# A gated linear attention with a ReLU feed-forward on one core: new issue orders, with one unit's y and two transposes ahead of the first gates

## The chip, the cores and the metric

The kernel runs on one core of a Trainium2 chip. The metric is the device time of one execution in microseconds (us); the time of a kernel is the median of its runs. The core's engines run side by side: TensorE (PE, with its weight loads as PEld), VectorE (DVE), ScalarE (ACT), GpSimd (POOL) and SyncE (SP), each with its own in-order queue of instructions, and transfers (DMA) that SP, ACT and POOL issue.

## What is computed

Four batches, eight heads, 768 positions, head size 48. The first half is a recurrence with a decay for each row of the state, the second a feed-forward with a ReLU gate over 3072 tokens of width 384 and a hidden width of 1536:

```python
def _attn_ref(q, k, v, f_logit):
    f = 1.0 / (1.0 + np.exp(-f_logit))
    state = zeros((B, H, D, D)); y = zeros_like(q)
    for t in range(S):
        state = f[:, :, t, :, None] * state + einsum('bhd,bhe->bhde', k[:, :, t], v[:, :, t])
        y[:, :, t] = einsum('bhd,bhde->bhe', q[:, :, t], state)
    return y

x = attn_out.transpose(0, 2, 1, 3).reshape(B * S, H * D)
gate = np.maximum(x @ w_gate, 0.0)
out = (gate * (x @ w_val)) @ w_out
```

## The kernel before

The recurrence is done in chunks of 128 positions. A step is one (chunk, batch) pair; 24 steps stand in six groups of four, written as group c = 0 to 5 and place b = 0 to 3. The first eight steps are paired into four units, which work on two neighbouring chunks of one batch at once, so places 0 and 1 of group 0 are one unit ("unit 0" by its number, with its two halves b = 0, 1; the steps b = 2, 3 of group 0 belong to the second unit; the change's own words call these steps unit 0's second half, and so does this text). For a step, in this order:

- the logits are loaded (L...f), ScalarE makes log(1 + exp(-f)) (`ef`, `ln`), TensorE sums it over positions with a triangular matrix (`cum`), ScalarE takes the exponentials (`ek`, `eq`) and the decay over the chunk (`dc`);
- GpSimd or VectorE multiply k and q with them, which gives the tensors `hats` (`hk`, `hq`). The first eight steps turn them on TensorE (`tk`, `tq`) and copy them from PSUM to SBUF (`ck`, `cq`); the others by transposing DMAs (`xh`);
- TensorE makes the scores (`s`), VectorE masks them (`m`), TensorE makes y within the chunk (`y`) and from the state (`yi` in a unit), and the chunk's share of the state (`kv`), which VectorE and GpSimd add and scale (`st`, `ss`, `sd`);
- y is copied into xT (`x`), or copied (`n`) and turned by DMA (`xx`), and is then the feed-forward's input.

The feed-forward works on a group of 512 tokens, the first one's first four hidden blocks on 256 tokens at a time. For hidden block j of 12, TensorE makes the gate (`g`) and the value (`u`) from slices of w_gate and w_val, ScalarE or VectorE the ReLU (`r`), VectorE the product (`p`); `o` are the output steps (four matmuls each), `d` their copies and `S` the stores. A name such as g02.1 is the gate of group 0 from place 2 on, block 1; u00.3 a value, o02.4 the output of place 2 over blocks 4 to 7. Weights are fetched in slices by DMAs that GpSimd issues: wg0+2 is w_gate's blocks 0 and 1, wv4+4 w_val's 4 to 7, wo4+8 w_out's 4 to 11. Loads of f, k, q and v are issued by SyncE, later ones also by ScalarE.

All of this is added to a plan as numbered operations, in one order; what runs when is set by tables. `ORDER` lists for each engine the numbers in the order of its queue (a negative entry ~12512 stands for 12 dummy matmuls of 512 columns that keep TensorE busy), `BANKS` gives the PSUM bank of each accumulation in TensorE's order, and `HELD` adds three waits by hand (69: 185 makes wv8+4 wait for relu r00.6). An operation's engine follows from the list it stands in. The waits are worked out from these lists: an engine waits for another only where data or a buffer asks for it, and everything behind a waiting instruction on its queue waits too.

```python
tenant, at = {}, 0
for op in self.order["PE"]:
    for t in op.opens:
        place = places[at]
        at += 1
        for o in tenant.get(place, ()):
            if op.deps.get(o, "order") == "order":
                op.deps[o] = "war"
        tenant[place], t.ap = t.ops, banks[place]
```

So a step that opens a bank waits for the last reader of that bank's tenant before it.

Of the kernel before, what the change touches and what calls it, by code (L numbers as in the profile page):

```python
# [25 lines left out]

ORDER = {
    "PE": [
        45, ~12512, 85, 74, ~2512, 90, ~2512, 121, 110, 80, ~2512, 82, 92, 95, 128, 101, ~9512, 116, 118, 266, 126,
# [14 lines left out]
    ],  # L44
    "ACT": [
# [9 lines left out]
    ],  # L55
    "DVE": [
# [11 lines left out]
    ],  # L68
    "POOL": [
# [4 lines left out]
    ],  # L74
# [5 lines left out]
    ],  # L80
}

# [2 lines left out]
}  # L85

BANKS = [
# [9 lines left out]
]  # L97


# [895 lines left out]
```

## Time and profile before

| | us |
|---|---|
| median of 3 runs | 191.91 (190.73 to 192.16) |
| the profiled execution | 190.59 |
| its span, first to last instruction | 188.9 |
| TensorE busy | 182.4 (97%) |
| VectorE busy | 133.9 (71%) |
| ScalarE busy | 91.9 (49%) |
| GpSimd busy | 60.7 (32%) |
| granted TensorE clock | 1.000 |

The profile is of one execution. The busy time of an engine leaves out its register, branch and DMA-issuing instructions; the end of a matmul is modelled, so that neighbouring matmuls overlap. DMA shares and landing times are of the core's 16 DMA engines. In the profile's rows, L842 is the gate and value matmul, L721 and L757 y of a unit, L699 its scores, L744 its state share, L601 the transposes, L589 and L590 the hats on GpSimd and VectorE, L443 the weight DMAs, L411 the loads of the units, L646 the copy to xT.

### The profile page before, as it was taken

What the parts mean: (1) busy time and instruction counts of PE and PEld (TensorE: products, weight loads), DVE (VectorE), ACT (ScalarE), POOL (GpSimd) and SP (SyncE); (2) the same over time, 40 slices, a digit from 0 to 9 for tenths busy, and PEclk for the clock granted to TensorE, in tenths of its full rate; (3) what the DMA queues carried; (4) which work ended last, traced back from release to release, by engine and by line L of the source; (5) the groups of instructions that cost most, each with busy time, mean ns of one, the idle gap of its engine ahead of it and who ended that gap; (6) DMA issues with size and microseconds to landing.
All of it is one profiled execution on the core that took longest, in us unless ns stands there. A gap on an engine that the chain in (4) does not pass through costs nothing.

```text
span 188.9 us, 4607 instructions
## 1 busy us (share of the span) xinstructions
PE 182.4 (97%) x1902; PEld 104.9 (56%) x1902; DVE 133.9 (71%) x246; ACT 91.9 (49%) x179; POOL 60.7 (32%) x88
## 2 busy tenths in 40 slices
PE   7989699999999999999999999999999999999994
PEld 3446486555545556555566555665555665555562
DVE  4476977988268879669776977997689954447802
ACT  3998746266882764866821648361425201240211
POOL 7099892600368210690018750126020000000000
PEclk9999999999999999999999999999999999999999
DMA  5999999997999999979899799795991120020223
GB/s 155 325 304 274 267 273 200 218 211 156 234 184 257 207 183 237 224 146 164 194 232 177 185 191 191 142 186 117 257 271 41 23 63 3 0 83 0 82 89 125
DMA packets 111045, 32.44 MB, mean 172 GB/s; under 512 B 104240, under 2 KB 110768, under 8 KB 111024
## 3 DMA queue, kind: packets, MB, share of 16 engines
q1 hardware_dynamic: 82128, 23.87, 58.2%
q10 hardware_dynamic: 25152, 4.73, 13.4%
q0 software_dynamic: 3744, 3.54, 11.3%
q8 instruction: 15, 0.25, 0.6%
q14 instruction: 6, 0.05, 0.1%
HBM read 25.95 MB, written 4.72 MB: 162 GB/s over the span
## 4 chain that ended last, share of the span: by engine, by line
PE 86%; DMA 6%; SPq 3%; POOL 2%; ACT 1%; issue 0%
PE ps L842 49%; PE ps L863 25%; DMA wg<-in_moe_w_gate_dram 3%; SPq L411 3%; DMA f_in<-in_f_logit_dram 3%; PE ps L633 2%; PE ps L795 2%; POOL hats L589 2%; PE ps L524 1%; PE ps L822 1%; PE ps L721 1%; PE ps L601 1%; PE ps L806 1%; PE ps L802 1%; PE ps L699 1%; PE ps L757 0%
## 5 line engine op out<-in xcount | busy, mean ns | idle before, releaser
L850 DVE TENSOR_TENSOR gT<-relu,ps 128x512 bf16<-128x512 bf16 (+1 forms) x76 | 48.0, 655 | 18.8 <-ACT relu L847 9.3
L842 PE MATMUL ps<-xT,wv 128*128 128x512 bf16 (+1 forms) x228 | 56.1, 368 | 0.0
L842 PE MATMUL ps<-xT,wg 128*128 128x512 bf16 (+1 forms) x228 | 54.7, 368 | 1.2 <-DMA wg<-in_moe_w_gate_dram 1.1
L863 PE MATMUL ps<-wo,gT 128*128 128x384 bf16 (+2 forms) x300 | 53.9, 320 | 0.0
L847 ACT ACTIVATE relu<-ps 128x512 bf16<-128x512 f32 (+1 forms) x47 | 26.7, 577 | 49.0 <-PE ps L842 46.7
L863 PEld LDWEIGHTS ps<-wo,gT 128*128 128x128 bf16 x300 | 28.1, 98 | 20.0
L842 PEld LDWEIGHTS ps<-xT,wg 128*128 128x128 bf16 x228 | 23.7, 108 | 21.3 <-DMA wg<-in_moe_w_gate_dram 1.5
L842 PEld LDWEIGHTS ps<-xT,wv 128*128 128x128 bf16 x228 | 23.5, 108 | 18.9
L848 DVE TENSOR_SCALAR relu<-ps 128x512 bf16<-128x512 f32 (+1 forms) x29 | 18.9, 658 | 9.7 <-PE ps L842 9.6
L589 POOL TENSOR_TENSOR hats<-k_in,expk 128x384 bf16<-128x384 f32 x17 | 16.9, 999 | 26.2 <-ACT expk L546 26.1
L589 POOL TENSOR_TENSOR hats<-q_in,expq 128x384 bf16<-128x384 f32 x15 | 17.8, 1190 | 19.0 <-ACT expq L548 12.5
L641 DVE TENSOR_TENSOR ptm<-ps,tri 128x512 bf16<-128x512 f32 x32 | 20.3, 683 | 2.3 <-PE ps L633 2.1
L869 ACT ACTIVATE osb<-ps 128x384 f32<-128x384 f32 (+2 forms) x18 | 8.6, 480 | 22.1 <-PE ps L863 20.7
L548 ACT ACTIVATE expq<-ps 128x384 f32<-128x384 f32 x24 | 15.5, 669 | 0.0
L468 POOL TENSOR_TENSOR st<-ssum,dec 128x384 bf16<-128x384 f32 x9 | 8.5, 945 | 19.5 <-DVE ssum L466 19.5
L546 ACT ACTIVATE expk<-ps 128x384 f32<-128x384 f32 x24 | 11.8, 498 | 2.0 <-PE ps L524 1.3
L493 ACT ACTIVATE f_in<-f_in 128x768 f32<-128x768 f32 x12 | 10.1, 840 | 2.7 <-DMA f_in<-in_f_logit_dram 2.6
L706 DVE TENSOR_TENSOR ptm<-ps,tmask 128x512 bf16<-128x512 f32 x16 | 10.3, 683 | 1.1 <-PE ps L699 1.1
L496 ACT ACTIVATE bneg<-f_in 128x768 bf16<-128x768 f32 x12 | 10.0, 840 | 0.9 <-ACT relu L847 0.7
L646 ACT ACTIVATE xT<-ps 128x384 bf16<-128x384 f32 x10 | 5.1, 535 | 9.6 <-PE ps L795 5.9
L619 POOL CAST vpad<-v_in 128x384 bf16<-128x384 f32 x12 | 6.9, 588 | 8.9 <-DMA v_in<-in_v_dram 8.9
L466 DVE TENSOR_TENSOR ssum<-ps,st 128x384 f32<-128x384 f32 x16 | 8.8, 551 | 0.7 <-PE ps L822 0.6
(76 smaller groups left out, 150.1 us busy)
## 6 DMA issues: line engine op xcount, KB each, us to landing
out_dram<-osb SPq DMA_DIRECT2D x23, 192.0 KB, 2.2
q_in<-in_q_dram SPq DMA_DIRECT2D x10, 384.0 KB, 5.4
f_in<-in_f_logit_dram SPq DMA_DIRECT2D x9, 384.0 KB, 5.3
v_in<-in_v_dram SPq DMA_DIRECT2D x9, 384.0 KB, 5.9
k_in<-in_k_dram SPq DMA_DIRECT2D x8, 384.0 KB, 5.9
k_in<-in_k_dram ACTq DMA_DIRECT2D x4, 384.0 KB, 6.0
f_in<-in_f_logit_dram ACTq DMA_DIRECT2D x3, 384.0 KB, 5.5
v_in<-in_v_dram ACTq DMA_DIRECT2D x3, 384.0 KB, 3.8
```

The source lines that it names most:

```text
L493: add(f"ef{c}{b0}", by("ACT", lambda: sc.activation(raw, raw, AF.Exp, scale=-1.0), act_(n)), keys, keys, key=P)
L496: add(f"ln{c}{b0}", by("ACT", lambda: sc.activation(bo, fl, AF.Ln, bias=1.0), act_(n)), keys + [f"bneg{bi}"], [f"bn{bi}_{x % 2}" for x in ...
L546: add(f"ek{c}{b}", by("ACT", lambda: sc.activation(ex[1], parts(bc.ap[:, 0:HD]), AF.Exp, scale=1.0), act_(HD)), [bc], [f"expk{ei}"], key=P ...
L548: add(f"eq{c}{b}", by("ACT", lambda: sc.activation(ex[0], parts(bc.ap[:, 0:HD]), AF.Exp, scale=-1.0), act_(HD)), [bc], [f"expq{eqi}_{b % 2 ...
L589: return {**by("POOL", lambda: gp.tensor_tensor(o, i_, e_, ALU.mult), pool_(HD)), **by("DVE", lambda: ve.tensor_tensor(o, i_, e_, ALU.mult ...
L641: add(f"m{c}{b}{j}", by("DVE", lambda b=b, j=j, mi=mi: ve.tensor_tensor(ptm[mi][:, j, :, :], s[b, j].ap[:, :].rearrange("p (n t) -> p n t" ...
L706: add(f"m{c}{b2[i]}{j}", by("DVE", lambda i=i, j=j, mask=mask: ve.tensor_tensor(ptm[mi[i]][:, j, :, :], s[j, i].ap[:, :].rearrange("p (n t ...
L842: z = te.matmul(bank.ap[:, 0:n], wt[:, kt, w_cols(j)], xT[xi][:, kt, n0:n1], start=(kt == 0), stop=(kt == NK - 1))
L847: add(f"r{c}{b0}.{j}", {**by("ACT", lambda: sc.activation(rdst, gate.ap[:, 0:n], AF.Relu), act_(n)), **by("DVE", lambda: ve.tensor_scalar_ ...
L848: **by("DVE", lambda: ve.tensor_scalar_max(rdst, gate.ap[:, 0:n], 0.0), dve_(n))}, [gate], [f"relu{ri}"], key=P)
L850: add(f"p{c}{b0}.{j}", by("DVE", lambda: ve.tensor_tensor(gT[gi][:, j, n0:n1], rdst, val.ap[:, 0:n], ALU.mult), dve_(n)), [val, f"relu{ri} ...
L863: z = te.matmul(o.ap[:, 0:e1 - e0], gT[gi][:, j, b * C:(b + 1) * C], wo[:, j, e0:e1], start=(j == 0), stop=(j == NJ - 1))
```

## The change

Only the tables change: the lists of all five engines in `ORDER` and the places in `BANKS`; `HELD`, the operations and their instructions stay, and so does the number of dummy matmuls (27). By the lists, 19 operations go from GpSimd to VectorE and 15 back, 5 from GpSimd to ScalarE and 4 back, 35 from VectorE to ScalarE and 35 back (copies and relus in the main), 5 DMA issues from SyncE to ScalarE and 6 back. The first rows of the table for TensorE show its kind:

```diff
     "PE": [
-        45, ~12512, 85, 74, ~2512, 90, ~2512, 121, 110, 80, ~2512, 82, 92, 95, 128, 101, ~9512, 116, 118, 266, 126,
...
+        45, ~12512, 85, 74, ~2512, 90, ~2512, 121, ~2512, 82, 92, 80, 110, 101, 95, 128, ~9512, 116, 230, 118, 266,
```

TensorE, where group 0's first gates start. Names in the rows are the tiles written and read: ps<-ptm,vpad is y within the chunk, ps<-qkT,st_0 its part from the state, ps<-ident,hats a transpose step, ps<-xT,wg a gate, ps<-xT,wv a value, ps<-bneg,ident a cum, ps<-vpad,hats the state share kv02. Before, from cum11 on:

```order
L513 MATMUL ps<-bneg,ident 128x384
L744 MATMUL ps<-vpad,hats 128x96 x16
L842 MATMUL ps<-xT,wg 128x256 x6
L601 MATMUL ps<-ident,hats 128x128 x4
L842 MATMUL ps<-xT,wv 128x256 x6
L513 MATMUL ps<-bneg,ident 128x384
L842 MATMUL ps<-xT,wg 128x256 x6
L721 MATMUL ps<-ptm,vpad 32x128 x64
L757 MATMUL ps<-qkT,st_0 32x128 x12
L601 MATMUL ps<-ident,hats 128x128 x8
```

and in the change (its lines are numbered one higher), from cum11 on, behind g00.2:

```order
L514 MATMUL ps<-bneg,ident 128x384
L843 MATMUL ps<-xT,wg 128x256 x3
L745 MATMUL ps<-vpad,hats 128x96 x16
L843 MATMUL ps<-xT,wv 128x256 x3
L602 MATMUL ps<-ident,hats 128x128 x4
L843 MATMUL ps<-xT,wv 128x256 x3
L514 MATMUL ps<-bneg,ident 128x384
L602 MATMUL ps<-ident,hats 128x128 x4
L722 MATMUL ps<-ptm,vpad 32x128 x64
L758 MATMUL ps<-qkT,st_0 32x128 x12
L602 MATMUL ps<-ident,hats 128x128 x4
L843 MATMUL ps<-xT,wg 128x256 x12
```

The first six gate matmuls before are g00.3 and g00.2 (slice wg2+2), the next six g00.0 and g00.1 (slice wg0+2). In the change y02, yi03 and the transposes tk11 and tk12 stand ahead of g00.1 and g00.0, which are followed by g02.2 and g02.1; kv02 stands behind the gates of slice wg2+2 and no longer ahead of them.

GpSimd, where the weights of blocks 4 to 11 are issued; the bracket is what the instruction waits for (d_q2_0 is the landing of Lq1.0, d_q3_0 of Lq1.2, e_ACT a step of ScalarE). Before:

```order
L443 DMA wv<-in_moe_w_val_dram 128x3x512
L589 TENSOR_TENSOR hats<-q_in,expq 128x8x48
L443 DMA wg<-in_moe_w_gate_dram 128x3x512
L332 MEMSET vpad 128x4x16
L443 DMA wo<-in_moe_w_out_dram 128x2x768
L589 TENSOR_TENSOR hats<-q_in,expq 128x8x48 [waits d_q2_0]
L443 DMA wv<-in_moe_w_val_dram 128x3x512 [waits e_ACT]
L443 DMA wo<-in_moe_w_out_dram 128x2x1536
```

and in the change:

```order
L444 DMA wv<-in_moe_w_val_dram 128x3x512
L590 TENSOR_TENSOR hats<-k_in,expk 128x8x48 [waits d_k3_0,e_ACT]
L590 TENSOR_TENSOR hats<-q_in,expq 128x8x48 [waits d_q3_0]
L590 TENSOR_TENSOR hats<-q_in,expq 128x8x48 [waits e_ACT]
L333 MEMSET tri 128x128
L590 TENSOR_TENSOR hats<-q_in,expq 128x8x48 [waits d_q2_0]
L444 DMA wg<-in_moe_w_gate_dram 128x3x512
L590 TENSOR_TENSOR hats<-q_in,expq 128x8x48
L444 DMA wo<-in_moe_w_out_dram 128x2x768
L444 DMA wv<-in_moe_w_val_dram 128x3x512 [waits e_ACT]
L444 DMA wo<-in_moe_w_out_dram 128x2x1536
```

wv4+4 is now issued ahead of the hats of unit 3, and the hats that wait for Lq1.0 (hq10) stand ahead of wg8+4, the next (hq11) ahead of wo0+4.

SyncE's loads of the units, before:

```order
L411 DMA k_in<-in_k_dram 128x8x96 x2
L411 DMA q_in<-in_q_dram 128x8x96
L411 DMA v_in<-in_v_dram 128x8x96
L411 DMA q_in<-in_q_dram 128x8x96
L411 DMA v_in<-in_v_dram 128x8x96
```

and in the change:

```order
L412 DMA k_in<-in_k_dram 128x8x96 x2
L412 DMA q_in<-in_q_dram 128x8x96 x2
L412 DMA v_in<-in_v_dram 128x8x96 x2
```

Lq1.0 is issued one place earlier, ahead of Lv1.2.

103 rows, old and new, of tables (BANKS, ORDER) are left out of this document.

## The prediction

> **What bounds the kernel now.** I first cut the span into stretches and read the table of busy time by stage, then the order of time on TensorE in the one stretch that shows idle time, then the chain that ended last, then the transfers.
>
> By stage (columns: start and end, length, then busy us and instruction count of PE, PEld, DVE, ACT, POOL, then the granted clock, DMA share and GB/s):
>
> ```profile
> 6.20:18.20 12.00, 11.02 (x220) 6.82 (x220) 7.63 (x18) 10.91 (x25) 8.78 (x11) 1.00 1.22 297
> 18.20:23.30 5.10, 3.43 (x69) 2.25 (x67) 4.75 (x9) 4.27 (x12) 4.60 (x8) 1.00 1.29 271
> 23.30:46.00 22.70, 22.64 (x374) 14.53 (x375) 19.01 (x37) 11.18 (x22) 9.14 (x13) 1.00 1.14 217
> 46.00:186.20 140.20, 140.17 (x1236) 79.55 (x1234) 100.13 (x162) 62.07 (x118) 34.78 (x37) 1.00 0.75 149
> ```
>
> From 46.00 to 186.20 TensorE is busy 140.17 of 140.20 us at a granted clock of 1.00: it is the bound, and an order that issues the same matmuls can gain nothing there, only lose. What is left behind 186.20 is the last copy and store. Idle time is left in two rows: 0.98 us in 6.20:18.20 and 1.67 us in 18.20:23.30. Before 18.20 TensorE fills its waits with dummy matmuls, whose number the change keeps (27), so the second row is the one to read closely. TensorE there:
>
> ```profile
> 19.48 0.52 PE L744 MATMUL ps<-vpad,hats 64*128 64x96 bf16 x16 [0.29 <-POOL vpad L619]
> 19.93 0.83 PE L842 MATMUL ps<-xT,wg 128*128 128x256 bf16 x6
> 20.97 0.38 PE L601 MATMUL ps<-ident,hats 128*128 128x128 bf16 x4 [0.21 <-POOL hats L589]
> 21.19 0.82 PE L842 MATMUL ps<-xT,wv 128*128 128x256 bf16 x6
> 21.85 0.33 PE L513 MATMUL ps<-bneg,ident 128*128 128x384 bf16 x1
> 23.30 0.83 PE L842 MATMUL ps<-xT,wg 128*128 128x256 bf16 x6 [1.13 <-DMA wg<-in_moe_w_gate_dram]
> ```
>
> The row at 23.30 is gates g00.0 and g00.1, the first users of weight slice wg0+2, which lands there: TensorE stood 1.13 us for it. The chain that ended last says the same, and gives lengths of single steps (start, us, what):
>
> ```profile
> 16.77 6.49 DMA wg<-in_moe_w_gate_dram
> ...
> 24.13 0.66 PE ps L721 x62
> 24.80 0.28 PE ps L757 x12
> ...
> 27.68 0.22 PE ps L601 x4
> 27.90 0.98 PE ps L842 x9
> ...
> 29.39 2.43 PE ps L842 x12
> 31.82 0.57 PE ps L699 x32
> 32.39 0.33 PE ps L601 x4
> 32.72 0.65 PE ps L842 x3
> ```
>
> So an intra-chunk y of a unit is 0.66 us, its state part 0.28, one transpose step 0.22 (the 0.33 row carries a change of mode besides), a 256-wide gate or value step 0.33 (0.98 for three), a score step of a unit 0.57, a 512-wide step 0.65.
>
> **Part 1: four steps in front of the first gates.** Behind cum13 (the row at 21.85) the change puts tk11, y02, yi03 and tk12 ahead of g00.1 and g00.0. They are 0.22 + 0.66 + 0.28 + 0.22 = 1.38 us of work that used to stand behind the wait. Whether they can run before wg0+2 lands at 23.25 is a question of their inputs. What feeds the steps before them, y00 and yi01, changes in one point: of the two k hats of unit 0's second half the first stays on GpSimd behind the same k load, the second goes to VectorE. Its cost is in the bound of part 3. GpSimd there:
>
> ```profile
> 15.98 0.84 POOL L468 TENSOR_TENSOR st<-ssum,dec 128x384 bf16<-128x384 f32 x1
> ...
> 20.83 0.99 POOL L589 TENSOR_TENSOR hats<-k_in,expk 128x384 bf16<-128x384 f32 x1
> 21.77 0.81 POOL L443 DMA_DIRECT2D wg<-in_moe_w_gate_dram  x1
> ```
>
> xT of unit 0 leaves ScalarE in two copies instead of one each on ScalarE and VectorE, whose rows are
>
> ```profile
> 17.86 0.60 ACT L646 ACTIVATE xT<-ps 128x384 bf16<-128x384 f32 x1
> 18.30 0.49 ACT L548 ACTIVATE expq<-ps 128x384 f32<-128x384 f32 x1
> ```
>
> with 0.44 us from start to start, so the second ends near 18.9 to 19.0. The first gate g00.2 can start at 19.0; before, gates started at 19.93 behind a state step that waited. From there: g00.2, cum11, g00.3, kv02 to about 20.4, u00.3 held for a bank until ScalarE has read cum11's sums, behind the two copies and four more steps of 0.4 (near 20.7), tk10 21.0, u00.2 21.2, cum13 21.5. tk11 needs the hats that end at 20.83 + 0.99 = 21.8 in both orders; y02 needs a bank that VectorE frees near 22.0; then 22.05 + 0.66 + 0.28 + 0.22 = 23.2. All four fit. Term: minus 1.38 at that point, with a small wait left.
>
> The next weight stops part of it. wg0+2 may be issued up to 0.45 us later, because the state product of the row at 15.98 now reads beside VectorE's hats; that shift is not priced, since the following slice, wg4+4, decides: the row at 21.77 (issue) and the landing times by transfer (line, queue, count, KB, us to landing) say 21.77 + 7.5 = 29.27.
>
> ```profile
> v_in<-in_v_dram SPq DMA_DIRECT2D x1, 384.0 KB, 8.5
> ...
> wg<-in_moe_w_gate_dram POOLq DMA_DIRECT2D x1, 384.0 KB, 7.5
> ...
> wg<-in_moe_w_gate_dram POOLq DMA_DIRECT2D x1, 384.0 KB, 8.2
> wo<-in_moe_w_out_dram POOLq DMA_DIRECT2D x1, 384.0 KB, 10.1
> ```
>
> Before, its first user g00.5 starts at 29.39 (the row of the chain). In the change g00.4 starts at 29.3, and s12 (0.57), tq10 (0.22) and u02.1 (0.33) have been done by then that were not: 1.12, and 0.1 for the start, so **minus 1.2 us** stands at 29.3.
>
> **Part 2: GpSimd's weight issues.** GpSimd before:
>
> ```profile
> 26.76 0.80 POOL L443 DMA_DIRECT2D wg<-in_moe_w_gate_dram  x1
> 27.56 0.17 POOL L332 MEMSET vpad<- 128x64 bf16 x1
> 27.65 0.74 POOL L443 DMA_DIRECT2D wo<-in_moe_w_out_dram  x1
> 28.93 0.99 POOL L589 TENSOR_TENSOR hats<-q_in,expq 128x384 bf16<-128x384 f32 x1 [0.54 <-DMA q_in<-in_q_dram]
> ```
>
> The change puts hq10, which waits for the q load of unit 2 (Lq1.0), ahead of wg8+4, and hq11 ahead of wo0+4; queued behind that wait are also wv8+4 and wo4+8, and who waits for them are gates 8 to 11 and the first output steps. SyncE issues that load one place earlier, in the place of a v load:
>
> ```profile
> 17.25 2.41 SPq L411 DMA_DIRECT2D v_in<-in_v_dram  x1
> 19.70 1.15 SPq L411 DMA_DIRECT2D q_in<-in_q_dram  x1
> ```
>
> The v load landed at 17.25 + 8.5 = 25.8; the q load before landed at 28.9, where the hats started. So hq10 finds its data when GpSimd comes to it, near 26.4 (hats of 1.0 each from 23.3 on), wg8+4 is issued near 27.4 (0.65 later than before) and wo0+4 near 29.2 (1.5 later). Need: g00.10 comes eight 512-wide steps, one transpose and one score step after 29.3: 29.3 + 5.2 + 0.22 + 0.67 = 35.4; o02.0 four steps later, 38.0. Upper end, if a landing follows its issue by the same time as before: wg8+4 at 27.4 + 8.2 = 35.6 (0.2 late), wo0+4 at 29.2 + 10.1 = 39.3 (1.1 later than 38.2): 1.3 us. Lower end: nothing, if the slices stand in line: before, these two were issued 0.9 us apart and landed at 35.0 and 37.7, 2.7 apart, so the second was waiting for the first and not for its issue. I take **plus 0.2**, near the lower end, since the gap of 2.7 against 0.9 is the nearest row.
>
> The Trainium skill, "DMA: Bandwidth & Descriptors", section "Queues, rings and completion order", says that on each DMA engine the descriptors of one ring are consumed in ring order while the engine takes turns between rings. By that rule a slice in a backlogged ring loses nothing by a later issue, and the sum would be 0.2 lower; the landings 2.7 us apart agree. That the weights' larger backlog (wv4+4 is issued right behind wg4+4) then takes turns from the q load is the same rule against this change; no run so far shows its size.
>
> wv8+4 and wo4+8 wait for r00.6 by a written hold; that relu moves forward with TensorE, so they are issued no later: nothing.
>
> **Part 3: the rest.** Exchanges of copies, relus and hats between VectorE, ScalarE and GpSimd (35 pieces each way between VectorE and ScalarE) lie beside a full TensorE. What hides them is the 140.17 us row; VectorE has 100.13 of 140.20 there, so 40 us of slack in the mean. Taken at nothing; if one arrives late, its lateness is added one to one. Upper bound by the nearest row: 1 us, the wait that one missing transfer caused at 23.30. The first stretch is also taken at nothing, between minus 0.5 (half of its 0.98) and plus 0.5 (one more hats on VectorE).
>
> **Sum.** The profiled execution took 190.59 (span 188.9 and 1.7 around it). 190.59 - 1.2 + 0.2 = 189.6. The runs shown have a median 1.3 above the profiled one, so I forecast **190.9** for a median. One per cent is 1.9 us, about what a measurement of this kernel can tell from no change; the whole idle time of 18.20:23.30 is less than that.
>
> **Rivals.** *A, slower: GpSimd stands at the q load in front of the weights.* If Lq1.0 lands when it did before (28.8), hq10 ends at 29.9, wg8+4 lands at 29.9 + 8.2 = 38.1, 2.7 late; hq11 and wo0+4 follow, issued at 31.7, landing at 41.8 against a need of 38.1 + 2.6 = 40.7, 1.1 more. 190.59 - 1.2 + 3.8 = 193.2, median 194.5. It outweighs the gain once hq10 starts after about 26.4, if landings follow issues. For it: the 0.54 us wait in the row at 28.93. Against it: the earlier place on SyncE. *B, the transfers hide the gain:* issue to landing stays 8.2 and 10.1, 1.3 us come back as waits for wg8+4 and wo0+4, 190.7, median 192.0. For it: wg0+2, which set the chain. Against it: 2.7 against 0.9. *C, faster:* all 1.67 us of the second row and half of the first's 0.98 go: 188.4, median 189.7. For it: all waits there lie on transfers or banks that the new order uses later. Against it: g00.2 still waits for xT, and wg4+4 for its landing.
>
> **How the numbers follow.** Forecast 0.52, B 0.20, A 0.15, C 0.13. C, which ends beyond the bound of 190.0, and the lower edge of the forecast give faster by over 1%: 0.16. Most of A, and a little for a stall that I have not seen, give slower by over 1%: 0.15. Within 1%: 0.69. The range runs from 189.2, below C, to 193.8, one per cent above the runs of before: it leaves out the far part of A and a little below C. The forecast's own range is 190.0 to 191.8.
>
> **What would show it.** Right: the 1.13 us wait in front of the first wg gate is under 0.5, with y and two transposes ahead of it; TensorE's idle time between 18.2 and 30 us falls by about 1; wg8+4's user starts by 35.6; 46 us to the end is as full as before, and ends 1 us earlier. Wrong: a wait of TensorE on DMA wg or wo between 35 and 42 us (B; A, with GpSimd idle on q_in ahead of it), or idle time of more than 0.5 us in any stretch behind 46 us, where I saw none.

## The result

The change has a median of 189.63 us (6 runs), against 191.38 for the kernel before in the 6 runs beside it; the ratio is 0.990, 95% interval 0.986 to 0.994. In a second set it was 189.62, ratio 0.990 (0.984 to 0.996). Ratios leave out executions more than 1.5% above the fastest of the same kernel, while medians hold them all.

The profiled execution took 189.74 (span 188.0), 0.85 less than the profiled 190.59 of before. The medians differ by 1.8. So there are two questions: whether the 0.85 is where the prediction put it, and where the other microsecond comes from.

The table of the change by stage (start and end, length, then busy us and count of PE, PEld, DVE, ACT, POOL, the clock, DMA share, GB/s):

```profile
6.20:18.20 12.00, 10.96 (x220) 6.89 (x222) 9.31 (x20) 11.21 (x26) 6.65 (x9) 1.00 1.22 302
18.20:23.30 5.10, 4.15 (x138) 3.04 (x134) 4.30 (x8) 4.39 (x13) 3.93 (x6) 1.00 1.27 267
23.30:46.00 22.70, 22.03 (x324) 14.49 (x320) 17.49 (x34) 12.42 (x25) 10.24 (x15) 1.00 1.08 207
```

TensorE's idle time in 18.20:23.30 fell from 1.67 to 0.95 us. From 18.2 to 30 us it fell from 1.73 to 1.09, less than the 1 us that the prediction named as its sign. The 0.67 of the third row must be read with care: this trace holds 1882 of the 1902 matmuls, and a missing first matmul of a step looks like 0.2 us of idle time. A profile with all 1902, shown further down, has none there. Behind 46 us TensorE shows no wait for another engine or a transfer in this trace, only three gaps of up to 0.2 us put down to "issue". TensorE itself:

```profile
19.32 0.50 PE L843 MATMUL ps<-xT,wg 128*128 128x256 bf16 x3 [0.53 <-ACT xT L647]
...
21.84 0.33 PE L514 MATMUL ps<-bneg,ident 128*128 128x384 bf16 x1
22.03 0.40 PE L602 MATMUL ps<-ident,hats 128*128 128x128 bf16 x4
22.36 0.60 PE L722 MATMUL ps<-ptm,vpad 64*32 64x128 bf16 x48
23.19 0.31 PE L722 MATMUL ps<-ptm,vpad 64*32 64x128 bf16 x16 [0.23 <-issue]
23.42 0.35 PE L758 MATMUL ps<-qkT,st 128*32 128x128 bf16 x12
23.71 0.40 PE L602 MATMUL ps<-ident,hats 128*128 128x128 bf16 x4
23.94 1.47 PE L843 MATMUL ps<-xT,wg 128*128 128x256 bf16 x12
...
28.63 0.64 PE L700 MATMUL ps<-qkT 48*64 48x128 bf16 x32
29.21 0.40 PE L602 MATMUL ps<-ident,hats 128*128 128x128 bf16 x4
29.75 1.89 PE L843 MATMUL ps<-xT,wg 128*128 128x512 bf16 x8
```

The four steps (rows at 22.03, 22.36, 23.42, 23.71) fill the place of the wait, and the gates behind them start at 23.94 with no wait in their row; slice wg0+2 had landed at 23.60. With the row at 29.21, which is tq10, the steps s12, tq10 and u02.1 are done. The first 512-wide gate stands at 29.75 with 8 of the 9 matmuls of three steps recorded, so it began one matmul (0.22) earlier, near 29.5, 0.1 behind the landing of wg4+4 (29.39). Before, that place was 29.39 with 1.12 us of these steps still to come: a gain of 1.0.

GpSimd's issues, where rival A saw the danger:

```profile
26.58 1.00 POOL L590 TENSOR_TENSOR hats<-q_in,expq 128x384 bf16<-128x384 f32 x1
27.52 0.80 POOL L444 DMA_DIRECT2D wg<-in_moe_w_gate_dram  x1
28.34 1.01 POOL L590 TENSOR_TENSOR hats<-q_in,expq 128x384 bf16<-128x384 f32 x1
29.29 0.76 POOL L444 DMA_DIRECT2D wo<-in_moe_w_out_dram  x1
```

hq10 does not wait, since Lq1.0 landed at 25.9 and not at 28.8. wg8+4 left 0.76 later than before and landed at 35.02 (before 35.00); wo0+4 left 1.64 later and landed at 37.27 (37.71). Their first users, g00.10 and o02.0, start at 35.6 and 38.2, with no wait.

### The profile page after: what moved, and what is told of

It is laid out like the page before. It is cut to its first block, busy times and chain, and to the rows that moved or that the text cites. A ratio compares the mean times of both kernels' runs of the same rounds, so it can differ in the third digit from the quotient of the medians.

```text
span 188.0 us, 4592 instructions
## 1 busy us (share of the span) xinstructions
PE 180.3 (96%) x1882; PEld 105.3 (56%) x1902; DVE 132.8 (71%) x250; ACT 93.6 (50%) x180; POOL 55.9 (30%) x83
## 4 chain that ended last, share of the span: by engine, by line
PE 86%; SPq 5%; DMA 4%; issue 2%; DVE 1%; POOL 1%; ACT 0%; POOLq 0%; DVEq 0%
PE ps L843 49%; PE ps L864 25%; SPq L412 5%; DMA k_in<-in_k_dram 4%; PE ps L634 2%; PE ps L796 2%; PE ps L525 1%; PE ps L722 1%; PE ps L823 1%; PE ps L602 1%; PE ps L807 1%; PE ps L803 1%; DVE gT L851 1%; POOL hats L590 1%; PE ps L758 0%
## 5 line engine op out<-in xcount | busy, mean ns | idle before, releaser
L851 DVE TENSOR_TENSOR gT<-relu,ps 128x512 bf16<-128x512 bf16 (+1 forms) x76 | 47.4, 654 | 20.6 <-PE ps L843 20.1
L843 PE MATMUL ps<-xT,wv 128*128 128x512 bf16 (+1 forms) x219 | 53.2, 368 | 1.2 <-issue 0.5
L843 PE MATMUL ps<-xT,wg 128*128 128x512 bf16 (+1 forms) x217 | 51.8, 367 | 1.4 <-ACT xT L647 0.5
L848 ACT ACTIVATE relu<-ps 128x512 bf16<-128x512 f32 (+1 forms) x51 | 28.4, 577 | 44.7 <-PE ps L843 34.4
L590 POOL TENSOR_TENSOR hats<-q_in,expq 128x384 bf16<-128x384 f32 x14 | 15.5, 1115 | 18.4 <-ACT expq L549 9.6
L849 DVE TENSOR_SCALAR relu<-ps 128x512 bf16<-128x512 f32 (+1 forms) x25 | 16.1, 651 | 5.9 <-PE ps L843 5.8
L469 POOL TENSOR_TENSOR st<-ssum,dec 128x384 bf16<-128x384 f32 x9 | 7.8, 870 | 27.2 <-DVE ssum L467 27.2
L871 DVE COPY osb<-ps 128x384 f32<-128x384 f32 x16 | 8.7, 552 | 9.6 <-PE ps L864 9.5
L870 ACT ACTIVATE osb<-ps 128x384 f32<-128x384 f32 (+2 forms) x9 | 4.0, 460 | 14.5 <-PE ps L864 9.3
L930 PE MATMUL ps<-zeros 128*128 128x512 bf16 x27 | 9.2, 492 | 0.0
```

Of the source, the lines that this page charges most:

```text
L590: return {**by("POOL", lambda: gp.tensor_tensor(o, i_, e_, ALU.mult), pool_(HD)), **by("DVE", lambda: ve.tensor_tensor(o, i_, e_, ALU.mult ...
L843: z = te.matmul(bank.ap[:, 0:n], wt[:, kt, w_cols(j)], xT[xi][:, kt, n0:n1], start=(kt == 0), stop=(kt == NK - 1))
L848: add(f"r{c}{b0}.{j}", {**by("ACT", lambda: sc.activation(rdst, gate.ap[:, 0:n], AF.Relu), act_(n)), **by("DVE", lambda: ve.tensor_scalar_ ...
L849: **by("DVE", lambda: ve.tensor_scalar_max(rdst, gate.ap[:, 0:n], 0.0), dve_(n))}, [gate], [f"relu{ri}"], key=P)
L851: add(f"p{c}{b0}.{j}", by("DVE", lambda: ve.tensor_tensor(gT[gi][:, j, n0:n1], rdst, val.ap[:, 0:n], ALU.mult), dve_(n)), [val, f"relu{ri} ...
```

## The experiments

Numbers in the diffs are the plan's numbers of operations; the sentence ahead of each says which they are. "Before" beside a run is the kernel before in the same set. All landing times are of the one profiled execution.

### The first gates back in front: `e1_gates_first` and `e1_again`

148 and 144 are g00.1 and g00.0; 246, 136, 140, 272 the four steps; 282 is tk13, 150 and 146 are u00.1 and u00.0; 279 is eq13, 143 the copy of yi03.

```diff
 PE    277,
-      246, 136, 140, 272, 148, 144, 168, 164, 282, 160, 172, 274, 150, 146,
+      148, 144, 246, 136, 140, 272, 282, 150, 146, 168, 164, 172, 274, 160,
 ACT   278,
-      247, 279,
+      279, 247,
 DVE   141,
-      143, 153, 145, 237, 155,
+      153, 145, 237, 155, 143,
```

> The change with gates g00.1 and g00.0 put back ahead of tk11, y02, yi03 and tk12; tk13, u00.1 and u00.0 follow these four, so that the gates g02 do not wait for the copies of y02 and yi03. Theory (the gain is the work done while slice wg0+2 is awaited): in the change cum13 ends near 21.9 and wg0+2 lands at 23.6, so TensorE stands 1.6 to 1.8 us there; 0.3 of it comes back at g00.4, which in the change waits 0.3 us for wg4+4 (landing 29.4). Time 1.0 to 1.4 us above the change (190.7 to 191.0 where the change has 189.6), and the first 512-wide gate starts near 31.0 instead of 29.75. Rival 1 (the gain came from GpSimd's issues or from the stretch behind 46 us): within 0.3 us of the change. Rival 2 (wg4+4 sets the place of the 512-wide gates whatever stands ahead of them): g00.4 starts by 30.0, time within 0.3 us.

Measured: 190.4 us, ratio to before 0.994 (0.992 to 0.997), so 0.8 us above the change's median, a little under the theory's lower end. The rows below are of a second run.

> The change with the two gates back ahead of the four steps, once more, for a profile at a granted clock of 1.00 (the first one lies at a lower clock). By the times (fast runs 190.2 to 191.7) the undone order costs 0.9 to 1.0 us. Theory: a wait of TensorE on DMA wg of 1.5 to 1.8 us between cum13 and g00.1, g00.4 starts near 30.8 and its wait for wg4+4 is gone. Rival: that wait is short and the time is lost in the copies of y02 and yi03 or at tk12.

Measured: 190.73, span 189.0, 1.0 above the change's. TensorE, and its busy time by stage:

```profile
21.86 0.33 PE L514 MATMUL ps<-bneg,ident 128*128 128x384 bf16 x1
23.80 0.82 PE L843 MATMUL ps<-xT,wg 128*128 128x256 bf16 x6 [1.61 <-DVE relu L849]
...
30.80 1.03 PE L843 MATMUL ps<-xT,wg 128*128 128x512 bf16 x4
```

```profile
30.00:46.00 16.00, 16.00 (x241) 9.25 (x241) 12.67 (x24) 8.24 (x15) 3.75 (x7) 1.00 1.15 207
46.00:120.00 74.00, 74.00 (x751) 41.60 (x750) 60.32 (x103) 39.43 (x69) 25.68 (x27) 1.00 1.07 204
```

The wait is back, 1.61 us, in front of g00.1. The row names a relu of VectorE that ends at 23.76, but g00.1 waits only for an older step of VectorE (done at 23.43) and for wg0+2, which landed at 23.66. g00.4 starts at 30.80, without a wait. Of the 1.61 us 1.3 are left at the first 512-wide gate (30.80 against 29.5) and 1.0 at the end; part of the difference is 0.4 us that the change's first profile lost inside y02 and this execution did not. So by the medians the four steps are worth 0.8 us. Single profiles give 1.0 against the change's first one and 1.7 against its second (span 187.3, at the end of this section). This trace holds all 1902 matmuls and shows the change's order full from 30 us on. And the kernel still stands 1.1 to 1.4 us below before in the medians, with the first gates waiting longer than in it: the rest of the gain is not there.

### Three of the four steps alone: `e2_three_ahead`

In the kernel before, 136, 140 and 246 (y02, yi03, tk11) go ahead of 144 and 148 (g00.0, g00.1), and 267 (ek12) ahead of 153 (a relu).

```diff
 PE    277,
-      144, 148, 136, 140, 282, 246,
+      136, 140, 246, 144, 148, 282,
 ACT   268,
-      153, 267,
+      267, 153,
```

> The kernel before with y02, yi03 and tk11 put ahead of g00.0 and g00.1 (tk12 can't be moved with them there: its hats come later), and ScalarE's ek12 one place earlier so that cum13 is ready; all else as before. Theory: the wait of 1.13 us for wg0+2 shrinks below 0.4, but the step that waits for wg4+4 (g00.5, landing 29.25, which before started at 29.39 with 0.2 us of wait) stays the first 512-wide gate with the same steps ahead of it. It starts at 29.3 to 29.4 again, the wait in front of it grows to about what was saved, and the time is that of before within 0.2 us. Rival (the wait for wg0+2 by itself was the loss): 0.9 to 1.1 us below before, ratio 0.995.

Measured: 192.05, before 191.79; ratio 1.004 (1.001 to 1.007). TensorE:

```profile
23.66 0.29 PE L721 MATMUL ps<-ptm,vpad 64*32 64x128 bf16 x12 [0.63 <-issue]
...
24.16 0.40 PE L601 MATMUL ps<-ident,hats 128*128 128x128 bf16 x4
24.40 0.82 PE L842 MATMUL ps<-xT,wg 128*128 128x256 bf16 x6
...
25.69 0.50 PE L842 MATMUL ps<-xT,wv 128*128 128x256 bf16 x3 [0.25 <-DVE gT L850]
...
29.04 0.61 PE L601 MATMUL ps<-ident,hats 128*128 128x128 bf16 x8
29.71 0.59 PE L842 MATMUL ps<-xT,wg 128*128 128x512 bf16 x2
```

The gates no longer wait for wg0+2, and nothing is gained; but this profile does not show the theory's way to that. TensorE stood 0.63 us inside y02, where the profile names nothing but "issue", and 0.25 us for VectorE behind the gates. So the transposes at 29.04 already lie 0.3 us behind their place in before (28.72). The first 512-wide gate begins near 29.5 (the row at 29.71 has 2 of its 3 matmuls), 0.1 behind its place in before, without a wait for wg4+4, which landed at 29.32. What shows the theory is a profile of a later experiment on before, `e9_load_on_sp`, in which wg0+2 happened to land 0.9 us earlier:

```profile
22.42 0.83 PE L842 MATMUL ps<-xT,wg 128*128 128x256 bf16 x6 [0.19 <-DMA wg<-in_moe_w_gate_dram]
...
29.46 0.81 PE L842 MATMUL ps<-xT,wg 128*128 128x512 bf16 x3 [0.63 <-DMA wg<-in_moe_w_gate_dram]
```

There the gates start 0.9 us earlier than in before, and the first 512-wide gate starts at 29.46 (29.39 in before), behind a wait of 0.63. What was saved in front of one slice was paid in front of the next. The change also brings steps ahead of that place which stood behind it (s12, tq10, u02.1); that this is why it gains is read from its rows, since no run moves these three alone.

### GpSimd's order: `e3_weights_first`, `e4_v_first`, `e5_q_last`

68 and 70 are wg8+4 and wo0+4, 235 and 245 hq10 and hq11. On SyncE 66 and 60 are Lq1.2 and Lq1.0, 67 and 61 Lv1.2 and Lv1.0.

```diff
 e3  POOL
-      235, 68, 245, 70,
+      68, 235, 70, 245,
 e4  SP
-      66, 60, 67, 61,
+      66, 67, 60, 61,
 e5  SP
-      66, 60, 67, 61,
+      66, 67, 61, 60,
```

> The change with GpSimd's slice wg8+4 put back ahead of hq10 and wo0+4 ahead of hq11: wg8+4 is issued near 26.6 instead of 27.5, wo0+4 near 28.4 instead of 29.3. Theory (the slices stand in line behind wv4+4): wg8+4 lands at 35.0 and wo0+4 at 37.3 again, within 0.3, and the time is that of the change within 0.2 us. Rival (a landing follows its issue): they land 0.9 us earlier, near 34.1 and 36.4; nobody waits for them there (g00.10 starts at 35.8, o02.0 at 38.2), so the time is the same too, but the landings tell the two apart. Where the hats that now stand behind the issues are late, tq10 or tq11 would show a wait on GpSimd and the time would rise by that.

> The change with SyncE's load Lv1.2 put back ahead of Lq1.0, which is the condition of the prediction's rival A. Lq1.0 is issued near 19.7 and lands near 28.8 as before, hq10 starts there, wg8+4 is issued near 29.9 instead of 27.5, wo0+4 near 31.7 instead of 29.3. Theory (slices stand in line): wg8+4 lands at 35.0 to 36.0 and the time rises by 0 to 0.4 us. Rival (landing follows issue by 7.5 and 8.0 us): wg8+4 at 37.4, g00.10 1.6 us late, wo0+4 at 39.7 just in time behind that; time 1.5 to 2.0 us above the change. Beside both: tq10 waits for hq10 at 29.2, up to 0.8 us, unless the later gates hide it.

> The change with SyncE's load Lq1.0 put behind Lv1.0, the last of the loads of units: a stronger form of the condition of rival A, since in the kernel with Lv1.2 ahead of it the load still landed at 27.0 and hq10 started only 0.5 us later. Lq1.0 is now issued near 21.0 and should land at 28.5 to 31. hq10 starts there, wg8+4 is issued 1.0 us later, at 29.5 to 32, instead of 27.5. Theory (slices stand in line): the slice loses little until its turn is missed; wg8+4 at 35.0 to 37.0, time 0 to 1.2 us above the change. Rival A as the prediction priced it (landing 7.5 to 8.2 us behind the issue): wg8+4 at 37.5 to 40, TensorE waits 1.7 to 4 us for it in front of g00.10, time up by that less 0.3. In both tq10, which needs hq10, waits 0 to 2 us at 29.2; that part is the wait for the hats, not for the weights.

Issue and landing of wg8+4, and the slice ahead of it (in before, hq10 is on VectorE, so its start does not hold back the issue there):

| | wv4+4 landed | hq10 started | wg8+4 issued | landed | behind the issue | behind wv4+4 |
|---|---|---|---|---|---|---|
| before | 32.58 | 30.90 | 26.76 | 35.00 | 8.2 | 2.4 |
| `e3` | 31.41 | 27.50 | 26.68 | 34.41 | 7.7 | 3.0 |
| the change | 31.99 | 26.58 | 27.52 | 35.02 | 7.5 | 3.0 |
| `e4` | 31.64 | 27.04 | 27.98 | 35.07 | 7.1 | 3.4 |
| `e5` | 32.57 | 29.30 | 30.24 | 36.71 | 6.5 | 4.1 |

`e3`: 189.52, ratio 0.989 (0.986 to 0.992), the same as the change. The slice left 0.84 earlier and kept its distance of 3.0 us to the slice ahead. It landed 0.6 earlier, where the theory had allowed 0.3 and the rival asked for 0.9; the slice ahead had landed 0.6 earlier too, so this profile alone does not tell the two apart. The order of hats and slices on GpSimd, the whole of part 2, costs nothing that these runs can tell.

`e4`: 189.97, ratio 0.993 (0.989 to 0.996), which does not separate from the change. The condition of rival A came about only in small: Lq1.0 landed at 26.97, and hq10 waited 0.61 us.

`e5` forced it. One of its four runs, the profiled one, took 191.27; the other three took 195.9 to 196.6, at a mean granted clock of 0.98 to 0.99, so what this order costs in time is not known. In the profiled run 1.3 us were lost in the first 20 us on another load (of k), so its time says little and the rows say more:

```profile
29.30 1.00 POOL L590 TENSOR_TENSOR hats<-q_in,expq 128x384 bf16<-128x384 f32 x1 [1.31 <-DMA q_in<-in_q_dram]
30.24 0.80 POOL L444 DMA_DIRECT2D wg<-in_moe_w_gate_dram  x1
```

```profile
39.89 1.46 PE L864 MATMUL ps<-wo,gT 128*128 128x384 bf16 x8 [0.29 <-DMA wo<-in_moe_w_out_dram]
```

Issued 2.7 us later than in the change, wg8+4 landed 1.7 later, of which 0.6 was in the slice ahead already, and TensorE waited 0.29 us, for wo0+4. It would have waited longer had it been on time: it reached g00.10 at 36.85 and not at 35.63. Against the users' starts in the change (35.6 and 38.2) wg8+4 was 1.1 us late and wo0+4, landed at 39.76, 1.5, so an estimate of what rival A's condition costs is 1.5 us; the hats of hq10, done at 30.30 where tq10 starts at 29.2 in the change, would account for 1.1 of it before the weights do. Over the whole table a later issue costs some, less than one to one: neither the line alone (nothing) nor the issue alone (everything). Rival A was right in its mechanism and too dear at 3.8 us.

### A slice earlier: `e7_best`

62 is wg4+4, 234 and 244 are hk10 and hk11; 410 is cum22, 210 and 220 are o00.8 and o02.8. The edit of `e3` is in it too.

```diff
 POOL  52,
-      234, 244, 62,
+      62, 234, 244,
 PE    209,
-      410, 292, 296, 210, 220, 385,
+      292, 296, 210, 220, 410, 385,
```

> The change with three small edits: wg4+4 is issued ahead of hk10, in 1.1 us in which GpSimd stands idle (18.8 to 19.9), 3.1 us earlier than in the change; wg8+4 and wo0+4 are issued ahead of hq10 and hq11; cum22, which waited 0.29 us for ln22, stands behind o02.8. Theory (a slice lands about 3 us behind the one ahead of it in line): wg4+4 lands 1 to 2 us earlier than 29.4 and the wait of 0.3 us in front of g00.4 goes, the wait in front of cum22 goes too: 0.4 to 0.6 us below the change, ratio to before 0.986. Rival 1: the earlier slice takes transfer time from the k and q loads of units 2 and 3, hats and transposes come later and the gain is lost: the same or up to 0.5 us above. Rival 2: wg4+4 lands at 29.4 whenever it is issued; only cum22's 0.3 us is gained.

Measured: 192.78, ratio 1.003 (0.999 to 1.007): the whole gain lost. The chain of this kernel, GpSimd and TensorE:

```profile
17.41 12.99 DMA q_in<-in_q_dram
```

```profile
30.48 0.98 POOL L590 TENSOR_TENSOR hats<-q_in,expq 128x384 bf16<-128x384 f32 x1 [3.83 <-DMA q_in<-in_q_dram]
```

```profile
31.61 0.38 PE L602 MATMUL ps<-ident,hats 128*128 128x128 bf16 x4 [2.63 <-POOL hats L590]
```

wg4+4 did land earlier, at 27.60. But Lq1.0, issued at the same time as in the change, took 13.0 us instead of 8.6 and landed at 30.40; hq10 followed, and TensorE waited 2.63 us for it at tq10. This is rival 1, and far dearer than the 0.5 us expected of it: the weight slice that went out earlier was paid by the load beside it. The other two edits have no part in it, since `e10_both` below holds them without this one and keeps the gain. The Trainium skill, "DMA: Bandwidth & Descriptors", section "Queues, rings and completion order", says that an engine goes round the rings that have work, packet by packet. The trace agrees in direction: more in GpSimd's ring, less for SyncE's.

### cum22 later, alone with `e3`: `e10_both`

The edits of `e7_best` without the one of wg4+4.

```diff
 POOL
-      235, 68, 245, 70,
+      68, 235, 70, 245,
 PE    209,
-      410, 292, 296, 210, 220, 385,
+      292, 296, 210, 220, 410, 385,
```

> The change with GpSimd's wg8+4 and wo0+4 back ahead of hq10 and hq11 (as in the earlier experiment, whose fast runs had a mean of 189.4) and cum22, which waited 0.29 us for ln22, behind o02.8. wg4+4 keeps its place. Theory: the wait in front of cum22 goes and nothing else moves; 0.2 to 0.4 us below the change, ratio to before near 0.988. Rival: o00.8 or o02.8 then waits for its product in the same place, or the transfer Lf2.2 was early enough anyway; the same as the change within 0.15 us.

Measured: 189.54, ratio 0.990 (0.985 to 0.994): as the change. By its time the rival holds: the 0.29 us in front of cum22 was not worth anything that can be measured. No version was found that beats the change.

Its profiled execution took 190.65, the slowest of its seven. VectorE and TensorE behind 46 us:

```profile
52.06 0.36 DVE L621 CAST vpad<-v_in 128x384 bf16<-128x384 f32 x1 [1.10 <-DMA v_in<-in_v_dram]
```

```profile
53.08 0.82 PE L843 MATMUL ps<-xT,wg 128*128 128x512 bf16 x3 [0.40 <-DVE relu L849]
```

A late load of v held VectorE for 1.10 us, and a gate waited 0.40 us for the relu behind it; at 59.22 a value step waits 0.45 us for another relu of VectorE. So the change's order, too, can meet a late transfer behind 46 us.

### The kernel before once more: `before_again`

> The kernel before, unchanged, for a second profile. Its profiled execution of 190.59 is among its fastest (25 runs: 190.43 to 192.75, median 191.8), while the change's 189.74 is near its median (189.6). Theory: in an execution of 191.5 or more the 1 us above the first profile is one or two waits for transfers that landed later than in the first (wg0+2 in front of g00.0 above 1.13 us, or wg4+4 in front of g00.5 above 0.2), waits whose place the change fills with other work. Rival: it is spread over the stretch behind 46 us (idle time there of 0.5 us or more, on loads of groups 2 to 5), and so has nothing to do with the four steps. If this execution is near 190.6 as well, it says nothing on this.

Measured: 192.25, span 190.5: 1.66 us above the first profile. By stage:

```profile
18.20:23.30 5.10, 3.39 (x67) 2.25 (x66) 4.65 (x9) 4.36 (x12) 4.52 (x9) 1.00 1.28 253
23.30:46.00 22.70, 22.42 (x372) 14.41 (x373) 19.14 (x37) 10.96 (x22) 9.05 (x13) 1.00 1.16 221
...
120.00:140.00 20.00, 19.08 (x168) 11.23 (x166) 15.23 (x28) 7.73 (x18) 5.45 (x6) 1.00 0.86 179
```

The first gates wait as in the first profile. 0.92 us of idle time is new, in 120 to 140. TensorE and the chain there:

```profile
133.39 0.82 PE L842 MATMUL ps<-xT,wg 128*128 128x512 bf16 x3 [0.92 <-DMA xT<-xn]
```

```profile
128.29 0.74 SPq L665
129.07 4.27 DMA xT<-xn
```

g40.1, the first gate of group 4, waits for xx40, the transposing DMA that brings the group's last quarter of x. It took 4.27 us; in the first profile 2.48, landing 1.05 us before its user. So for this execution the theory written down was wrong and its rival right: 0.92 of its 1.66 us lie at one place behind 46 us. What differs is the distance to the load Lk5.2, which ScalarE issues behind it:

| | xx40 issued | Lk5.2 issued | between | xx40 took |
|---|---|---|---|---|
| before | 128.20 | 129.23 | 1.03 | 2.48 |
| `e2_three_ahead` | 128.97 | 129.87 | 0.90 | 2.48 |
| `before_again` | 129.07 | 129.81 | 0.74 | 4.27 |
| `e8_cover` | 128.63 | 129.33 | 0.70 | 4.31 |

### Covering that wait: `e8_cover`

728 is g40.1, 618 is u30.9.

```diff
 PE    616,
-      728, 618, 724,
+      618, 728, 724,
```

> The kernel before with one value step, u30.9, put ahead of gate g40.1 (they stand side by side; nothing else moves). In the second profile of before (192.25) 1.1 of the 1.7 us above the first profile lie at g40.1, which waits 0.92 us for the transposing transfer of x (issue to landing 4.27 us instead of 2.48). Theory (this late transfer is what makes most executions of before slower than its first profile): 0.65 us of work now covers the wait, so the median falls by about 0.65, from 191.8 to 191.1 or 191.2, with the fastest executions unchanged near 190.5; ratio 0.996 to 0.997. Rival (the wait at g40.1 was a chance of that one execution, and the slower executions have other causes): median within 0.2 us of before.

Measured: 191.78, before 191.56; ratio 1.002 (0.999 to 1.005). By its time this is the rival. None of its 12 runs lies below 191.20, though the fastest were expected to stay near 190.5. Its profile (191.2, its fastest run) shows the wait all the same, shorter by the cover:

```profile
132.98 1.25 PE L842 MATMUL ps<-xT,wg 128*128 128x512 bf16 x5 [0.35 <-DMA xT<-xn]
```

Why its other runs are not 0.65 us faster than those of before stays open.

### Taking the other load away from it: `e9_load_on_sp`

797 is Lk5.2, 680 is xx40.

```diff
 ACT   685, 838, 679,
-      797, 617,
+      617,
 SP    720, 686, 680,
-      814,
+      797, 814,
```

> The kernel before with one load, Lk5.2 (k of the last group), moved from ScalarE's queue to SyncE's, directly behind the transposing DMA xx40. The change has this load on SyncE too. In four profiles of before and its two variants, xx40 took 2.48 us where ScalarE issued Lk5.2 0.90 or 1.03 us behind it, and 4.27 to 4.31 us where it was 0.70 or 0.74 us behind; in the latter g40.1 waited (0.92 us in the second profile of before, 0.35 us with 0.65 us of other work in front). Theory (a race of the load's packets with xx40 makes the slower executions of before): on SyncE the load follows 1.3 to 1.5 us behind xx40, xx40 takes 2.5 us, no wait at g40.1 in the profile, and the median falls by 0.7 to 1.0 us to 190.7 to 191.0, ratio 0.995 to 0.997. Rival (the slower executions have other causes, the race is one of several): xx40 takes 2.5 us and g40.1 does not wait, but the median stays within 0.3 us of before.

Measured: 190.9, before 191.93: 1.0 lower in the median. The ratio is 0.997 (0.994 to 1.000), at the edge of what these runs resolve, so that no change at all is not excluded; by the means it is 0.6 lower. 8 of 12 runs lie between 190.65 and 191.05; of the 76 runs of before that the ratios of all sets rest on, 26 lie below 191.2. SyncE and TensorE:

```profile
130.19 0.58 SPq L421 DMA_DIRECT2D k_in<-in_k_dram  x1
```

```profile
131.36 1.46 PE L842 MATMUL ps<-xT,wg 128*128 128x512 bf16 x6
```

xx40 was issued at 128.89 and took 2.40 us; g30.9 and g40.1 run through without a wait. The move is one that the change contains: it issues Lk5.2 on SyncE too.

### The change once more: `after_again`

> The change, unchanged, beside the two others on the same chip, and for a second profile. Theory: it has no wait of more than 0.4 us behind 46 us in this execution either, so its time lies within 0.5 us of its first profile (189.74), and the difference of the medians to before (1.8 to 2.2 us) is the 0.9 of the four steps plus about 1 us of late transfers behind 46 us that only before's order meets. Rival: an execution of 190.5 or more with a wait of its own behind 46 us, so that the difference is one of chance.

Measured: the profiled execution took 189.09, the median 189.62. It has no wait above 0.4 us behind 46 us, but its time lies 0.65 below the first profile, outside the 0.5 of the theory. The rows show most of that ahead of 30 us:

```profile
22.27 0.74 PE L722 MATMUL ps<-ptm,vpad 64*32 64x128 bf16 x64
...
29.23 1.89 PE L843 MATMUL ps<-xT,wg 128*128 128x512 bf16 x8
```

y02 runs through, without the 0.4 us lost inside it in the first profile; wg4+4 landed at 28.85, and the first 512-wide gate (again with its first matmul unrecorded) began near 29.0 instead of 29.5. TensorE's idle time from 18.2 to 30 us is 0.77 here, about 1 less than in before. That only before's order meets late transfers behind 46 us is not borne out: `e10_both` shows one in the change's order.

In the first profile of the change xx40 and xx41 landed at 129.23 and 130.41, 1.2 us and more before the step that reads them at 131.58.

## Why the prediction was right, and where it was not

**Part 1 held.** 1.2 us were forecast at 29.3; by the steps done at the first 512-wide gate it was 1.0 in the change's first profile and 1.5 in its second, and by undoing it 0.8 in the medians. The single times were near: hats done at 21.97 (21.8 forecast), the fourth step done at 23.9 (23.2), the 512-wide gate near 29.5 (29.3). g00.2 came at 19.32 instead of 19.0, and 0.4 us were lost inside y02, where the profile names nothing but "issue". wg0+2 was issued 0.47 us later, which the prediction had seen (up to 0.45) and left without a price, and landed at 23.60; the four steps were done 0.3 behind that, so no wait was left. That the next slice stops the gain is shown by the rows of `e9_load_on_sp`. Three steps ahead of the gates (`e2_three_ahead`) brought nothing, but in the profile their gain was lost ahead of that slice.

**Part 2 was dearer in the forecast than on the chip.** Plus 0.2 was taken between 0 and 1.3; as far as `e3_weights_first` can tell it was 0. The times of issue came out as forecast (27.5 for 27.4, 29.3 for 29.2), and there was no wait behind them.

**The sum** of 189.6 for the profiled execution stands beside 189.74. That they meet so closely is in part luck, since a second execution of the change took 189.09.

**The step that failed is the last one:** "The runs shown have a median 1.3 above the profiled one, so I forecast 190.9". The median of 189.63 lies below the forecast's own range of 190.0 to 191.8. The 1.3 was taken for something that any order carries along; between the change's median and its first profile it is nothing (189.63 and 189.74). At least part of it belongs to before's own order: in its first profile xx40 landed 1.05 us ahead of its user, in the second its user waited 0.92 us for it. With Lk5.2 issued elsewhere the median of before falls by 1.0, to 0.3 above the first profile, though the interval of that ratio just reaches no change. The change moves this load as well. No run puts it back on ScalarE in the change, so that this is where the change's other microsecond comes from is argued and not shown. The prediction's opening said of the stretch from 46 us on that an order "can gain nothing there, only lose". That was read from one execution, and that one was among the fastest.

**The rivals.** B: no wait for wg8+4 or wo0+4, it fell. A: its condition did not arise; forced, the landings put it at about 1.5 (estimated above) and not at 3.8. C named the time that came (189.7), by a reason that did not: 0.95 us of idle time stays in 18.2 to 23.3. That its time was met is luck.

What stays open: how the 1.0 us of slower executions of before divides among places. One profile shows 0.92 at g40.1 and 0.7 spread over smaller delays; the cover of 0.65 us did not bring the median down, while moving the load did.

## What to carry to other kernels

A median that lies a microsecond above its profile can be a wait that this profile does not show: take a second profile before adding the difference to a forecast, and look at transfers that land less than their own spread ahead of their user. Work put in front of a wait for a transfer counts only up to the next transfer, so the same steps must pass that one too. A transfer issued earlier on one queue can be paid on another, as in `e7_best`: price the loads beside it.

## What the runs showed of the hardware

The transposing DMA xx40 took 2.48 us where a 384 KB load on another queue was issued 0.90 or 1.03 us behind it, and 4.27 and 4.31 us where it was 0.74 and 0.70 behind; with the load 1.30 us behind it on its own queue it took 2.40. That a load issued later can go with a delay of 1.8 us was not expected; these are five profiles, and one of them moved the load on purpose. The Trainium skill, "DMA: Bandwidth & Descriptors", section "Queues, rings and completion order", says that a completion lands only after every earlier write of that engine, across its queues. A load whose packets run ahead of xx40's last ones could delay it that way; no run here shows that, or separates it from the engine's taking turns.

In one execution the granted clock fell behind one late load. In the first profile of `e1_gates_first`, of 195.34 us, a k load landed 7.78 us behind its issue (4.88 in the change), at 17.8, and TensorE stood 3.30 us for its hats:

```profile
19.30 0.40 PE L602 MATMUL ps<-ident,hats 128*128 128x128 bf16 x4 [3.30 <-POOL hats L590]
```

```profile
14.00:18.20 4.20, 2.01 (x11) 0.69 (x8) 2.56 (x6) 2.74 (x4) 0.60 (x2) 1.00 1.22 258
18.20:20.00 1.80, 0.70 (x12) 0.57 (x13) 0.46 (x2) 0.00 (x0) 1.80 (x2) 1.00 1.25 247
20.00:22.00 2.00, 2.00 (x47) 1.46 (x50) 0.82 (x4) 1.39 (x5) 1.98 (x4) 0.54 0.91 243
22.00:24.00 2.00, 2.00 (x108) 1.47 (x92) 0.83 (x2) 1.75 (x6) 0.61 (x1) 0.61 1.07 170
```

The clock (third column from the end) was 0.54 and 0.61 over the next 4 us. The late load and the clock together moved the first copy of x from 18.23 (in the change) to 22.94.
